# Another order of all operations, and another choice of engine for many of them, in a fused attention and MLP kernel

## The chip, the cores and the metric

One core of one Trainium2 chip runs the whole program. The metric is the device time of one execution in microseconds. The kernel before takes 373.58 us, the median of 4 runs that lie between 371.93 and 376.04 us.

## What is computed

```python
def _attn_ref(q, k, v):                       # each (8, 12, 448, 64), float32
    scores = np.matmul(q, k.transpose(0, 1, 3, 2)) / np.sqrt(64)
    attn = np.maximum(scores, 0.0) ** 2 / 448
    return np.matmul(attn, v)

def _moe_ref(x, w_in, w_out):                 # (3584, 768), (768, 2048), (2048, 768)
    h = x @ w_in
    g = h * (1.0 / (1.0 + np.exp(-1.702 * h)))
    return g @ w_out
```

The attention has no softmax: a relu, a square, a constant. Its output, with the heads side by side, is the `x` of the MLP, and the output is float32, 3584 x 768.

## The kernel before, in words

The work on the matrices is done in float16 with float32 sums. The attention runs in 24 **units** (8 batches x 3 groups of four heads). A unit is loaded as float32 by SP (`Lk`, `Lq`) and cast (`K`, `Q`), or loaded with a cast by a DMA that POOL issues (`jk`, `jq`, `V`). Its k and q are transposed by TensorE and copied out of PSUM (`tk`, `ek`, `tq`, `eq`; units 0 to 5) or by a DMA (`Rk`, `Rq`; the others). Then come 7 blocks of scores (`s`, four matmuls of 64x64 into two PSUM banks), for each block two relus out of PSUM (`r`) and one square (`x`), and the product with v (`a`, 28 matmuls). Its result is copied out of PSUM into the transposed x of the MLP (`e`).

The MLP runs in 8 **groups** of alternately 384 and 512 tokens, each as soon as its tokens are there. Its first product is plain (`f`) for group 0 and for half of group 1; elsewhere it is one level of a Strassen scheme of seven half-size products (`u`), for which sums of the inputs (`T`) and of the weights (`S`) are made on VectorE. Each result goes through a copy out of PSUM (`t`) or a sum with one (`b`), a gelu on ScalarE (`g`), and a scaling into float16 on POOL (`v`). The second product is plain (`m`, group 0), or Strassen in pairs of 128 tokens (`p`, with `A` and `W` for the sums), or single for an odd one (`i`). Its results are copied or added into the output tile (`n`, `h`, `l`), which SP stores (`o`).

**What sets the order.** There is no scheduler at work: the function ends with a list of some 1,930 words, and `do` (from L436) issues one after the other. A word names an operation, its numbers, optionally an engine (`:a` ScalarE, `:d` VectorE, `:p` POOL, else the operation's home) and PSUM banks or buffers (`@3.4`). So `x1.1:p` is the square of unit 1, block 1, on POOL. Each engine takes its own words in the order of the list and waits at each until its inputs and its buffer are there; nothing overtakes. Eight PSUM banks, three buffers for relu results (`rl0` to `rl2`), eight for squares (`at`), five for gelu inputs (`gf`) tie the engines together: a score block can't start before the last reader of its two banks is done.

**Lines that matter.** L88 is the helper `tt` for all two-input operations (squares `at<-rl`, sums); L79 to L85 is the helper `copy` (casts, copies, evictions); L104 the DMAs that POOL issues for q, k and v; L131 transposes; L150 scores; L161 and L163 relu on VectorE and on ScalarE; L169 the square on ScalarE; L182 the product with v; L204 the products `u`, `p`, `i`, `m`; L215 gelu; L218 the scaling on POOL; L405 and L409 the weights' DMAs; L453 ten matmuls on zeros at the start, while the first loads are under way.

Of the kernel before, what the change touches and what calls it, by code (L numbers as in the profile page):

```python
# [15 lines left out]
def kernel(  # L16
# [9 lines left out]
    nc = tc.nc  # L26
# [390 lines left out]
    with tc.manual_schedule():  # L417
# [31 lines left out]
        zero = new("gf", [128, 1024], F16, "zero")  # L449
        nc.vector.memset(zero[:, 0:512], 0.0)  # L450
        zp = bank([7], "zp")
        for _ in range(10):
            nc.tensor.matmul(out=zp, lhsT=zero[:, 0:128], rhs=zero[:, 0:512],  # L453
                             start=True, stop=True)
        words = (
            "I Lk0 K0:d tk0@0 jk1 Lq0 Q0:a jq1 V1 V0 ek0 tq0@1 jk2 tk1@2 eq0 s0.1@3.4 s0.0@5.6 "
            "ek1 r0.1.1@0 s0.3@7.0 r0.1.0:d r0.3.1@1 tq1@1 r0.3.0:d s0.4@2.4 r0.0.0@2 s0.5@3.0 "
            "x0.1 x0.3 s0.2@7.5 r0.0.1 x0.0 r0.4.0@0 r0.4.1 s0.6@6.2 r0.5.0:d@1 x0.4 r0.6.1@2 eq1 "
            "jq2 tk2@4 s1.0@3.2 r0.5.1 r0.6.0 x0.6 r0.2.1@0 x0.5 r0.2.0 x0.2 ek2 r1.0.0@2 r1.0.1 "
            "x1.0 s1.1@0.6 r1.1.1@1 s1.2@1.5 tq2@7 eq2 r1.2.1:d@0 jwa1 jq3 r1.2.0 jk4 jk3 r1.1.0 "  # L460
            "s1.3@3.2 a0@6.4 jwa0 jwb0 r1.3.1@2 s1.4@1.0 r1.3.0 e0.0.1:a jwb1 x1.3 e0.1.1 jq4 "
            "x1.2:a tq3@7 s1.6@2.5 r1.6.1@2 s2.0@3.4 eq3 e0.0.0 V2 s1.5@7.5 r1.6.0 e0.1.0 "
            "s2.2@6.2 jwa3 r1.4.0:d@0 x1.1:p x1.6 jwb3 r1.4.1 x1.4 tk3@1 ek3 r1.5.1@1 r1.5.0 "
            "r2.0.0@2 tk4@0 r2.0.1 x1.5 s2.3@5.7 r2.3.1@0 s2.1@3.1 r2.3.0 V3 r2.2.0@1 ek4 x2.0 "
            "r2.2.1 r2.1.0@2 a1@4.7 r2.1.1:d x2.3 e1.0.0 s2.5@5.0 r2.5.1:d@0 jq5 e1.0.1:a e1.1.1 "
            "x2.2:a x2.1:p jk5 s2.4@6.2 f0.0.0@1 f0.2.0@3 r2.5.0 f0.2.1 f0.0.1 e1.1.0 s2.6@0.7 "
            "x2.5 s3.0@5.4 r2.4.1@1 f0.3.0@2 r2.4.0 r2.6.0@2 r2.6.1 f0.3.1 jwa2 r3.0.0:d@0 x2.4 "
            "f0.1.0@6 s3.1@0.5 r3.0.1 r3.1.1@1 f0.4.0@7 G3 Lk6 f0.1.1 x2.6 a2@4.5 r3.1.0:d x3.0:p "
            "tq4@0 S1.1 e2.0.0 x3.1 f0.4.1 e2.0.1:a f0.2.2 f0.3.2 e2.1.1 g0.2 jwb2 g0.3 f0.1.2 "
            "e2.1.0:a g0.1 eq4 f0.0.2 s3.4@5.3 s3.3@0.2 r3.4.0:d@2 g0.0 f0.5.0@4 r3.4.1 r3.3.0@0 "  # L470
            "V4 f0.4.2 f0.5.1 g0.4 v0.4 s3.2@6.1 r3.2.1@1 r3.2.0 r3.3.1:d x3.4 x3.3 s3.5@5.3 "
            "s3.6@2.0 f0.5.2 f0.6.0@7 f0.6.1 r3.6.1:d@2 r3.6.0 Lq6 r3.5.0@0 f0.7.0@1 x3.2 r3.5.1 "
            "x3.6 tk5@6 s4.1@0.2 g0.5 s4.0@5.3 r4.1.0@1 v0.1 jo0.1 f0.7.1 f0.7.2 v0.3 f0.6.2 "
            "r4.0.0@2 x3.5 r4.0.1:d ek5 r4.1.1 g0.6 x4.0 v0.5 s4.3@4.0 s4.2@5.3 S0.1 a3@2.6 "
            "r4.3.0@0 s4.4@7.4 g0.7 V5 r4.2.1@2 r4.2.0:d r4.3.1:d tq5@1 e3.0.0:a x4.3 x4.1 "
            "e3.0.1:a x4.2 S0.2 s4.6@3.5 r4.4.0@0 s4.5@0.2 f0.9.0@6 f0.9.1 r4.6.1@1 f0.9.2 eq5 "
            "r4.5.0:d@2 f0.12.0@7 f0.8.0@5 f0.12.1 f0.12.2 r4.6.0:d r4.4.1 f0.10.0@4 f0.10.1 v0.7 "
            "f0.10.2 v0.0 x4.6 r4.5.1 s5.3@2.1 g0.12 g0.9 s5.0@0.7 jo1.0 x4.4:p g0.10 r5.0.0@0 "
            "s5.2@3.6 r5.2.1@1 r5.0.1 x5.0:a f0.8.1 f0.8.2 x4.5 v0.10 r5.3.1:d@2 a4@4.0 e4.0.0:a "
            "s5.6@1.6 v0.12 f0.15.0@7 f0.15.1 f0.15.2 g0.8 r5.3.0:d r5.2.0:d r5.6.1@0 v0.9 S1.2 "  # L480
            "x5.3 r5.6.0:d s5.4@2.3 e4.0.1 s5.1@4.5 g0.15 x5.6:a s5.5@1.6 r5.1.0@2 r5.1.1:d "
            "f0.13.0@0 f0.13.1 f0.13.2 S2.1 S2.2 x5.2:a jo0.0 f0.14.0@7 r5.5.0@0 v0.8 x5.1:p "
            "f0.11.0@5 f0.14.1 f0.14.2 f0.11.1 Q6:d jo1.1 f0.11.2 r5.5.1:d r5.4.1:d@1 r5.4.0 "
            "f1.1.0@4 g0.13 x5.4 f1.5.0@1 v0.2 v0.6 v0.15 f1.1.1 x5.5 f1.5.1 K6:p S2.3 g0.11 "
            "f1.3.0@2 f1.2.0@0 a5@5.6 g0.14 Lk7 e5.0.0:a f1.6.0@3 f1.6.1 f1.0.0@7 e5.0.1:a f1.5.2 "
            "g1.5 S2.4 f1.4.0@5 S3.1 T1.1 T1.2 S3.2 W0.1 v0.14 v0.13 v1.5 f1.4.1 u1.3.0@6 t1.3.0 "
            "f1.1.2 S3.4 Rq6 v0.11 T1.4 g1.1 K7 f1.3.1 f1.4.2 f1.3.2 f1.2.1 f1.2.2 V6 W1.1 W1.2 "
            "W3.1 f1.0.1 f1.0.2 g1.0 u1.2.0@1 t1.2.0 Lq7 u1.3.1@4 v1.1 u1.2.1@7 g1.4 v1.0 b1.2.1 "
            "u1.3.2 Q7:a m0.0.0@5 f1.6.2 g1.2 Rk6 v1.2 b1.3.1 S1.4 W2.1 S0.3 S3.3 Lq8 g1.3 V7 Lk8 "
            "g1.6 Rk7 u1.2.3 v1.4 v1.6 n0.0.0 Rq7 s6.1@0.2 W3.2 s6.0@5.3 r6.0.1@2 W2.2 Q8 "  # L490
            "r6.0.0:d u1.3.3 r6.1.1:d@1 r6.1.0:d u1.2.2 s6.2@3.5 K8:p f1.7.0@2 g1.3.1 v1.3.1 "
            "x6.0:a g1.2.1 r6.2.1:d@0 f1.7.1 f1.7.2 v1.2.1 r6.2.0:d T1.3 t1.3.2 W2.4 t1.2.2 "
            "m0.0.1@0 g1.7 x6.1:a u1.2.4 S1.3 x6.2 s6.4@5.3 n0.0.1:a r6.4.0@2 s6.3@2.0 v1.7 W0.2 "
            "Lq9 t1.2.4:d b1.2.3 v1.3 Rq8 r6.4.1 x6.4 r6.3.1@1 r6.3.0 u1.3.4 t1.3.4:d u1.2.5 "
            "g1.2.5 u1.2.6 Q9 s6.5@5.3 r6.5.1:d@0 s6.6@0.2 x6.3:a b1.2.6 b1.3.3 r6.6.0@2 r6.6.1 "
            "x6.6:a g1.2.6 v1.2.6 m0.1.0@1 Lk9 s7.1@3.0 Rk8 Lq10 s7.0@7.2 r6.5.0:d x6.5 n0.1.0:a "
            "r7.1.0:d@1 r7.0.1@2 K9:p r7.1.1:d r7.0.0 g1.3.3 u1.3.6 b1.3.6 u1.3.5 x7.0 s7.2@5.1 "
            "W3.4 s7.3@3.2 v1.2.5 g1.3.5 r7.2.0@0 r7.2.1 g1.3.6 a6@0.7 g1.2.3 v1.2.3 v1.3.5 "
            "e6.0.1:a s7.4@4.6 r7.3.1:d@2 Lk10 K10:p x7.1 s7.5@5.1 x7.2:a m0.1.1@2 Q10:d e6.0.0 "
            "V11 e6.1.0:a e6.1.1:a r7.4.0@1 r7.3.0:d v1.3.6 r7.4.1 Rq9 r7.5.1@0 r7.5.0:d x7.5:a "  # L500
            "x7.3 x7.4 Rk9 s7.6@0.7 s8.1@3.4 n0.1.1:a r7.6.1@2 s8.0@5.6 r8.0.0:d@1 r7.6.0:d x7.6 "
            "m0.2.0@1 Lq11 r8.1.1:d@0 s8.2@5.2 s8.3@0.7 r8.1.0 o0.1 a7@3.4 r8.0.1 x8.0 r8.3.0@2 "
            "r8.3.1 v1.3.3 A1.0.1@0 r8.2.1@1 V8 V10 Lk11 r8.2.0:d x8.1:a s8.4@6.0 e7.0.0 x8.3 "
            "e7.1.0:a r8.4.0@0 s8.5@7.5 e7.0.1:a Q11 r8.5.0@2 x8.2 A1.0.2@1 r8.4.1 e7.1.1:a "
            "r8.5.1:d x8.5 n0.2.0:a m0.2.1@2 s8.6@3.6 s9.1@7.5 Rk10 r8.6.1@1 x8.4 r9.1.1@2 "
            "s9.0@0.4 r9.0.1@0 p1.0.0@1 n0.2.1:a h1.0.0 r9.0.0 Lq12 s9.3@6.5 r8.6.0:d x8.6 "
            "r9.3.0@1 Rq10 r9.1.0:d W0.3 a8@3.4 s9.2@2.7 r9.3.1 x9.1:a s9.4@0.6 e8.0.1:a K11:d "
            "e8.0.0 W1.3 x9.0 p1.0.2 r9.4.1@2 u2.1.0@5 r9.2.0@0 T2.1 Q12 t2.1.0 T2.2 W1.4 e8.1.1 "
            "u2.0.0@6 u2.1.1@2 b2.1.1 W2.3 T2.3 r9.2.1:d e8.1.0:a t2.0.0 r9.4.0 x9.4:a u2.1.2 "
            "u2.0.2 u2.2.0@3 t2.0.2 u2.0.1@4 g2.1.1 Rq11 t2.1.2 b2.0.1 u2.2.1@0 v2.1.1 g2.0.1 "  # L510
            "v2.0.1 u2.0.4 t2.0.4 o0.2 T2.4 u2.0.3 t2.2.0 S0.4 u2.1.4 b2.0.3 b2.2.1 u2.1.3 g2.2.1 "
            "g2.0.3 u2.0.6 u2.2.2 u2.3.0@7 o0.0 u2.0.5 b2.0.6 u2.3.1@4 t2.1.4:d v2.2.1 b2.1.3 V9 "
            "x9.3:a g2.0.6 u2.1.6 u2.1.5 v2.0.3 u2.2.3 t2.2.2 v2.0.6 t2.3.0:d Lk12 b2.1.6 b2.3.1 "
            "h1.0.2:d Lq13 g2.1.3 v2.1.3 g2.0.5 g2.1.6 v2.0.5 g2.3.1 u2.2.4 v2.1.6 g2.1.5 u2.3.3 "
            "u2.3.2 t2.2.4:d x9.2:a b2.2.3 u2.2.5 v2.3.1 v2.1.5 t2.3.2 A1.0.3 W3.3 u2.2.6 g2.2.5 "
            "b2.2.6 W0.4 u2.3.4 t2.3.4 b2.3.3 s9.6@6.2 r9.6.1:d@2 s9.5@5.3 r9.5.0:d@1 p1.0.1@0 "
            "A1.0.4 r9.6.0 g2.3.3 u2.3.6 V12 r9.5.1 s10.0@6.2 r10.0.1:d@0 b2.3.6 x9.6:a l1.0.1 "
            "s10.1@3.5 g2.2.6 r10.1.1@2 Rk11 K12 u2.3.5 p1.0.4 v2.2.5 r10.0.0 r10.1.0 Rk12 Rq12 "
            "p1.0.3 g2.3.5 x9.5 s10.3@2.4 h1.0.4 A1.2.1@1 A1.2.2@0 a9@5.6 r10.3.0:d@1 r10.3.1:d "
            "x10.0:a l1.0.3 s10.2@3.7 e9.0.1 x10.3:p x10.1:a Q13 r10.2.1@0 p1.0.5 Lk14 l1.0.5:a "  # L520
            "s10.6@2.4 r10.6.1@2 r10.2.0:d s10.5@6.7 p1.0.6 r10.5.1@1 e9.0.0:a r10.5.0:d v2.3.3 "
            "r10.6.0:d x10.2:a A1.2.3 l1.0.6 x10.5 o1.1 s11.0@3.1 o1.0 r11.0.0@0 r11.0.1 "
            "s11.3@4.6 s10.4@7.2 r10.4.1@1 p1.2.0@5 x10.6 p1.2.1@0 s11.2@3.1 x11.0 Lq14 r10.4.0 "
            "x10.4 h1.2.0:d r11.3.0@2 r11.2.0:d@0 r11.3.1 r11.2.1 K14:d Lk15 V16 A1.2.4 s11.1@2.7 "
# [140 lines left out]
```

## Time and profile before

| | |
|---|---|
| median of the runs | 373.58 us |
| the profiled execution's own time | 376.04 us |
| its span, first to last instruction | 374.3 us |
| TensorE (PE) busy | 359.2 us, 96% |
| VectorE (DVE) busy | 305.2 us, 82%, 532 instructions |
| ScalarE (ACT) busy | 270.3 us, 72%, 536 instructions |
| GpSimd (POOL) busy | 172.3 us, 46%, 222 instructions |
| mean granted TensorE clock | 0.987 |

The profiled execution is the slowest of the four runs, 2.46 us over the median. Busy time of PE is to be read with care: the ends of matmuls are modelled, and a matmul that waits inside a busy stretch isn't seen as idle. On the other engines, busy time is the union of the instructions' intervals; neighbours overlap a little, so that the durations of a row add up to more.

### The profile page before, as it was taken

The numbers are of one execution on the slowest core, as the hardware profiler recorded it, in microseconds if no ns is written. First come the engines' busy times: TensorE is split into PE (matmuls) and PEld (weight loads), VectorE is DVE, ScalarE is ACT, GpSimd is POOL, SyncE is SP. The second block draws the span as 40 slices with busy tenths as digits, with TensorE's granted clock in tenths as the row PEclk, the third lists the DMA queues.
The fourth block names the chain that finished last, engine by engine and source line by source line (L and its number), as shares of the span: only waits on it lengthen the run. The fifth ranks groups of instructions, "written<-read, shape, count | busy, mean of one in ns | idle before, by whom it ended". The sixth has DMA issues, their size and how long they took to land.

```text
span 374.3 us, 9188 instructions
## 1 busy us (share of the span) xinstructions
PE 359.2 (96%) x3566; PEld 233.1 (62%) x3566; DVE 305.2 (82%) x532; ACT 270.3 (72%) x536; POOL 172.3 (46%) x222
## 2 busy tenths in 40 slices
PE   7869999999899999999999999999999999999993
PEld 3445554655469555885579655786558855588652
DVE  4998999899998996988979878887799699455741
ACT  3867994579898989867787768769977766566311
POOL 6645768554506238376435743046322733114400
PEclk9889999999999999999999999999999999999998
DMA  8999999995998498458772482849173340401224
GB/s 188 191 195 223 205 159 197 207 203 126 208 210 174 68 218 171 98 124 211 165 142 90 102 191 53 167 139 167 26 226 76 49 110 3 109 2 45 63 64 127
DMA packets 64908, 51.39 MB, mean 137 GB/s; under 512 B 35680, under 2 KB 61280, under 8 KB 64864
## 3 DMA queue, kind: packets, MB, share of 16 engines
q1 hardware_dynamic: 48256, 36.71, 40.7%
q0 software_dynamic: 16608, 14.09, 26.5%
q8 instruction: 28, 0.46, 0.5%
q14 instruction: 16, 0.13, 0.2%
HBM read 45.61 MB, written 11.01 MB: 151 GB/s over the span
## 4 chain that ended last, share of the span: by engine, by line
PE 80%; DVE 11%; issue 2%; ACT 2%; DMA 2%; POOL 1%; DVEq 0%; POOLq 0%; ACTq 0%
PE ox L204 27%; PE hx L204 23%; PE sc L150 8%; PE av L182 7%; PE ht L229 6%; PE os L204 4%; DVE at L88 3%; DVE rl L161 2%; PE op L204 2%; DMA q<-in_q_dram 2%; DVE gf L88 2%; ACT rl L163 1%; PE tr L131 1%; DVE wT L88 1%; DVE wout L88 0%
## 5 line engine op out<-in xcount | busy, mean ns | idle before, releaser
L163 ACT ACTIVATE rl<-sc 128x448 f16<-128x448 f32 x219 | 107.2, 550 | 22.1 <-PE sc L150 13.9
L161 DVE TENSOR_SCALAR rl<-sc 128x448 f16<-128x448 f32 x117 | 68.8, 615 | 8.4 <-PE sc L150 7.2
L218 POOL TENSOR_SCALAR go<-gf 128x512 f16<-128x512 f32 x64 | 43.1, 673 | 64.8 <-ACT gf L215 53.0
L88 DVE TENSOR_TENSOR at<-rl 128x896 f16<-128x896 f16 x97 | 65.2, 694 | 3.5 <-ACT rl L163 2.2
L88 POOL TENSOR_TENSOR at<-rl 128x896 f16<-128x896 f16 x22 | 38.4, 1749 | 52.9 <-ACT rl L163 23.0
L204 PEld LDWEIGHTS <-win 128*128 128x128 f16 x624 | 56.9, 98 | 7.3 <-issue 1.8
L88 DVE TENSOR_TENSOR gf<-hx,gf 128x512 f32<-128x512 f32 (+1 forms) x78 | 47.3, 624 | 15.7 <-PE hx L204 9.3
L150 PE MATMUL sc<-qT,kT 64*64 64x448 f16 x672 | 50.4, 366 | 4.5 <-DVE xo L83 2.5
L218 POOL TENSOR_SCALAR ge<-gf 128x384 f16<-128x384 f32 x64 | 36.4, 569 | 34.0 <-ACT gf L215 30.4
L215 ACT ACTIVATE gf<-gf 128x512 f32<-128x512 f32 (+1 forms) x78 | 43.4, 577 | 7.8 <-DVE gf L88 7.5
L169 ACT ACTIVATE at<-rl 128x896 f16<-128x896 f16 x49 | 46.3, 951 | 3.3 <-DVE rl L161 2.9
L204 PEld LDWEIGHTS <-winS 128*128 128x128 f16 x468 | 42.8, 98 | 5.2 <-issue 1.5
L204 PE MATMUL ox<-wout,go 128*128 128x384 f16 x256 | 46.0, 326 | 0.0
L204 PEld LDWEIGHTS <-go 128*128 128x128 f16 x320 | 30.0, 98 | 23.8 <-issue 5.2
L79 ACT ACTIVATE gf<-hx 128x512 f32<-128x512 f32 (+1 forms) x54 | 28.8, 545 | 16.7 <-PE hx L204 13.7
L204 PEld LDWEIGHTS <-ge 128*128 128x128 f16 x288 | 27.0, 98 | 21.3 <-issue 4.8
L182 PE MATMUL av<-at,v 64*64 64x448 f16 x672 | 37.5, 354 | 0.0
L204 PE MATMUL hx<-T,winS 128*128 128x256 f16 (+1 forms) x312 | 35.9, 260 | 0.2
L150 PEld LDWEIGHTS <-kT 64*64 64x64 f16 x672 | 17.6, 106 | 27.0 <-issue 21.8
L204 PE MATMUL ox<-wT,asum 128*128 128x384 f16 x176 | 31.6, 326 | 0.0
L204 PE MATMUL hx<-xo,win 128*128 128x256 f16 x252 | 31.3, 273 | 0.1
L182 PEld LDWEIGHTS <-v 64*64 64x64 f16 x672 | 20.7, 109 | 12.8 <-issue 2.8
(78 smaller groups left out, 481.8 us busy)
## 6 DMA issues: line engine op xcount, KB each, us to landing
out_dram<-osb SPq DMA_DIRECT2D x56, 192.0 KB, 3.3
kst<-in_k_dram SPq DMA_DIRECT2D x19, 448.0 KB, 4.7
qst<-in_q_dram SPq DMA_DIRECT2D x19, 448.0 KB, 4.3
v<-in_v_dram POOLq DMA_DIRECT2D x24, 224.0 KB, 5.7
win<-in_moe_w_in_dram POOLq DMA_DIRECT2D x8, 384.0 KB, 8.9
wout<-in_moe_w_out_dram POOLq DMA_DIRECT2D x4, 768.0 KB, 8.2
k<-in_k_dram POOLq DMA_DIRECT2D x5, 224.0 KB, 6.1
q<-in_q_dram POOLq DMA_DIRECT2D x5, 224.0 KB, 6.8
```

The lines of the kernel that those rows point to most:

```text
L79: nc.scalar.activation(out=o, in_=i, func=AF.Copy)
L88: eng[e].tensor_tensor(out=o, in0=x, in1=y, op=op)
L131: nc.tensor.matmul(out=ps[64 * a:64 * a + 64, j * 128:(j + 1) * 128], lhsT=x[:, a, 64 * j:64 * j + 64], rhs=ident[:, :], is_transpose=True)
L150: nc.tensor.matmul(out=sc[a][c, 0:S], lhsT=st["kT"][r, j, c], rhs=st["qT"][r, :, c], start=True, stop=True)
L161: nc.vector.tensor_scalar(out=o, in0=i, scalar1=0.0, scalar2=None, op0=ALU.max)
L163: nc.scalar.activation(out=o, in_=i, func=AF.Relu)
L169: nc.scalar.activation(out=at, in_=rl, func=AF.Square)
L182: nc.tensor.matmul(out=av[s][64 * a:64 * a + 64, 0:S], lhsT=v16[r, a, 64 * j:64 * j + 64], rhs=at[r, a, :], start=(j == 0), stop=(j == J - 1))
L204: nc.tensor.matmul(out=o, lhsT=lhs(i), rhs=rhs(i), start=start and i == 0, stop=i == n - 1, skip_group_check=True)
L215: nc.scalar.activation(out=o, in_=i, func=AF.Gelu_apprx_sigmoid, scale=1.0 / SC)
L218: eng[e].tensor_scalar(out=o, in0=i, scalar1=SC, scalar2=1.0, op0=ALU.mult, op1=ALU.mult)
L229: nc.tensor.matmul(out=hp[g, f][:, 0:n], lhsT=w[:, i, fo:fo + 128], rhs=xts[g][:, i, 0:n], start=i == 0, stop=i == NK - 1)
```

## The change

The change replaces the list of words. The two lists hold the same operations, with the same numbers, 1,931 words before and 1,933 after; all of them stand in another order, nearly all PSUM banks and relu buffers differ, and 342 operations go to another engine. Most of these moves cancel each other; what is left of them, by kind:

| operation | VectorE | ScalarE | POOL |
|---|---|---|---|
| `K`, cast of k | 5 to 1 | 5 to 7 | 9 to 11 |
| `Q`, cast of q | 5 to 1 | 3 to 9 | 11 to 9 |
| `x`, square | 97 to 92 | 49 to 53 | 22 to 23 |
| `r`, relu | 117 to 115 | 219 to 221 | |
| `t`, copy out of `hx` | 24 to 28 | 54 to 50 | |
| `e`, x of the MLP | 32 to 31 | 40 to 41 | |
| `h`, `l`, `n`, output | 53 to 55 | 36 to 34 | |

The two words that are new are `z13@0` and `z1`: the zero matmuls, now 14 of 384 columns in place of 10 of 512, of which the last stands after the first transposes. They read a part of the tile `wT[2]`, which is written much later. The core of the diff:

```diff
-        zero = new("gf", [128, 1024], F16, "zero")
-        nc.vector.memset(zero[:, 0:512], 0.0)
-        zp = bank([7], "zp")
-        for _ in range(10):
-            nc.tensor.matmul(out=zp, lhsT=zero[:, 0:128], rhs=zero[:, 0:512],
-                             start=True, stop=True)
+        zero = wT[2][:, 0, :]
+        nc.vector.memset(zero, 0.0)
+        zp = []
+
+        def zeros(e, p, n):
+            if p:
+                zp.append(bank(p, "zp"))
+            for _ in range(n):
+                nc.tensor.matmul(out=zp[0][:, 0:NOUT], lhsT=zero[:, 0:128], rhs=zero,
+                                 start=True, stop=True)
+
+        two["z"] = zeros
         words = (
-            "I Lk0 K0:d tk0@0 jk1 Lq0 Q0:a jq1 V1 V0 ek0 tq0@1 jk2 tk1@2 eq0 s0.1@3.4 s0.0@5.6 "
...
-            "s2.2@6.2 jwa3 r1.4.0:d@0 x1.1:p x1.6 jwb3 r1.4.1 x1.4 tk3@1 ek3 r1.5.1@1 r1.5.0 "
...
-            "f0.11.0@5 f0.14.1 f0.14.2 f0.11.1 Q6:d jo1.1 f0.11.2 r5.5.1:d r5.4.1:d@1 r5.4.0 "
...
+            "z13@0 jk1 Lk0 K0:d Lq0 Q0:a I jq1 V1 tk0@1 z1 ek0 tq0@2 tk1@3 jk2 jq2 eq0 s0.3@4.5 "
+            "V0 ek1 s0.1@6.7 s0.0@0.1 r0.3.1@0 tq1@2 s0.4@3.5 r0.0.0@1 r0.3.0:d s0.2@4.0 r0.1.1@2 "
...
+            "r1.1.1:d a0@6.5 x1.0 jwb0 x1.2 e0.0.1:a e0.0.0 s1.5@1.4 s1.6@0.7 jq4 x1.1 r1.5.1@2 "
...
+            "f0.5.1 v0.0 f0.5.2 f0.8.1 f0.8.2 r3.6.1:d v0.3 jwb3 r3.5.1 x3.5:a s4.2@6.5 s4.1@7.4 "
+            "r4.0.1:d x3.6 a3@3.2 r4.1.1@1 r4.2.0:d@0 r4.2.1 jo1.1 g0.5 V4 r4.1.0:d x4.1 s4.3@6.4 "
...
```

The DMAs that POOL issues, in the order of its queue up to the third unit's v: before `jk1 jq1 V1 V0 jk2 jq2 jwa1 jq3 jk4 jk3 jwa0 jwb0 jwb1 jq4 V2`, after `jk1 jq1 V1 jk2 jq2 V0 jk3 jq3 V2`. The last quarter of the first weight (`jwb3`) stands before ahead of `x2.1:p`, and after behind `x3.0:p v0.1 v0.0 v0.3`.

## The prediction

> **What bounds the kernel now.** I read the page's slices first:
>
> ```profile
> PE   7869999999899999999999999999999999999993
> ...
> DVE  4998999899998996988979878887799699455741
> ...
> PEclk9889999999999999999999999999999999999998
> ```
>
> TensorE idles visibly in the first three slices (28 us) and the last; DVE is at nine tenths through the first third. The windows show the same in numbers (columns: window, its length, busy us and instruction counts of PE, PEld, DVE, ACT, POOL, granted clock, DMA share, GB/s):
>
> ```profile
> 10.00:20.00 10.00, 7.17 (x111) 3.62 (x104) 9.25 (x13) 7.82 (x17) 7.58 (x10) 0.83 1.22 189
> 20.00:30.00 10.00, 8.45 (x102) 4.74 (x102) 9.05 (x20) 8.13 (x18) 5.22 (x7) 0.83 1.24 199
> ...
> 50.00:110.00 60.00, 58.16 (x530) 32.86 (x520) 57.29 (x91) 45.67 (x90) 31.23 (x39) 1.00 1.02 180
> 110.00:370.00 260.00, 257.76 (x2517) 177.40 (x2514) 206.16 (x369) 187.91 (x369) 109.56 (x139) 1.00 0.51 115
> ```
>
> DVE is 95% busy up to 110 us, 79% after it. PE's busy time hides waits, so I priced each word by its streaming rate in the chain of waits (start, length, what):
>
> ```profile
> 137.93 1.32 PE av L182 x28
> ...
> 193.29 12.38 PE hx L204 x150
> ...
> 352.89 15.65 PE ox L204 x96
> ```
>
> That is 0.163 us for a matmul of 384 columns, 0.082 for one of 192 (0.107, between the two, for 256), 1.31 us for an `a`, 0.19 for a score block. All words sum to 329.7 us. The 374.3 us span is then 5.6 before the first transpose, 329.7, about 33.0 of gaps (start of one word to start of the next, less its price), and a tail of 5.8. The gaps: 13.9 us before 50 us, 6.4 from 50 to 110, 12.8 in the remaining 258 us, which is 0.5 in 10 us, mostly 0.1 at each change from scores to another product. So **up to 110 us the kernel is paced by VectorE, and after that by TensorE**. The largest gap, 3.0 us at 18.4, has this around it in the timeline:
>
> ```profile
> 17.28 3.57 DVE L88 TENSOR_TENSOR at<-rl 128x896 f16<-128x896 f16 x1 [0.41 <-ACT rl L163]
> ...
> 18.62 1.74 POOL L88 TENSOR_TENSOR at<-rl 128x896 f16<-128x896 f16 x1
> ...
> 21.04 0.38 PE L150 MATMUL sc<-qT,kT 64*64 64x448 f16 x3 [2.31 <-DVE xo L83]
> ```
>
> A square that takes 0.62 us undisturbed takes 3.57; it ends just after POOL's square, and PE then waits 2.31 for a copy queued behind it.
>
> **What the skill says.** The Trainium skill, "SBUF — State Buffer", section "Who interferes with whom": VectorE and GpSimd share a port pair under an exclusive lock; a VectorE instruction with two SBUF inputs collides with a GpSimd one that reads SBUF, and casts and copies in their two-port modes collide with any. The trace agrees: 3.57 against 0.62 above, and `Q6:d` at 54.39 took 2.10 against a row of 1.085 with POOL's square beside it. Instructions stretched by over 0.25 us lose 10.1 us in all before 110 us. "TensorE: Matmul & The Clock Gate", Part 1: too little work halves the clock for a while; here it was 0.83 in both windows from 10 to 30 us and full before and after. "Perfetto Trace Analysis", "Optimizing Scalar/DVE Operations": a duration includes an end that overlaps with the next instruction. So it is: 11 ScalarE relus in a row took 5.25 us, 0.477 each against a row of 0.550 (factor 0.87).
>
> **The change, part by part.**
>
> *Engines.* Rows: casts of k on DVE 0.637, ACT 0.944, POOL 1.017; of q 1.085, 0.950, 0.962; squares 0.62 (undisturbed), 0.951, 1.749; relus 0.615, 0.550; `t` 0.62, 0.54 over both sizes; output copies 0.55, 0.49. DVE: -4x0.637 - 4x1.085 - 5x0.62 - 2x0.615 + 4x0.62 + 0.55 = **-8.1 us**. ACT: 2x0.944 + 6x0.950 + 4x0.951 + 2x0.550 - 4x0.54 - 0.5 = **+9.8**. POOL: 2x1.017 - 2x0.962 + 1.749 = +1.9. On PE nothing: 14x384 against 10x512 zero columns, under the wait for the first loads (k's cast ends at 5.0).
>
> *Order.* I summed the rows of each engine's words ahead of three places in each list:
>
> | ahead of | PE | DVE | ACT | POOL |
> |---|---|---|---|---|
> | `a1` | 9.2, 9.0 | 18.2, 17.2 | 18.9, 18.5 | 15.3, 10.7 |
> | `u2.0.0` | 83.8, 85.9 | 102.7, 101.8 | 95.9, 100.7 | 62.0, 56.7 |
> | the end | 329.7, 329.7 | 327.0, 318.6 | 311.2, 321.2 | 172.8, 174.6 |
>
> (before, after). In the trace `a1` starts at 24.9 us, and group 2's first product at 109.2.
>
> 1. **Up to `a1`: -3.0 us.** `x1.1` leaves POOL, whose first square is now unit 3's, so nothing like the 3.57 us block stands in the list. DVE would have 2.95 us less to wait, and 1.0 less to do. Also V0 moves behind `jk2` and `jq2`: the first POOL loads land some 1.1 us apart (10.34, 11.44, 12.57), so k of unit 2, for which `tk2` waited until 12.6 us with 2.1 us of gap, should land a place sooner, near 11.4. What is late next is the draining of PSUM: 14 relus a unit on two engines. Between 0 and -4.
>
> 2. **`a1` to `u2.0.0`: -1.0 us, and 2.1 us of PE work more done.** DVE's rows in between are 84.5 before and 84.6 after, and it took 84.3 us: the pace stays. ACT's grow from 77.0 to 82.2, at 0.87 some 71.5: under DVE. What remains of the stretched instructions is 7.1 us; fewer DVE casts and POOL squares (5 down to 1 before unit 6) should take a part: 0 to -3. As 2.1 us more of products are issued by then, and PE has room (86 in 105 us), the part behind is shorter by **2.1**.
>
> 3. **POOL's queue: +0.5 us.** `jwb3`, which landed at 31.82 before, now waits for `x3.0:p` and three scalings, the last behind the gelu `g0.3`. That puts its issue near 36 us (PE work 19 to 20 in the order; before, 38 us, less step 1) and its landing, with 2 us a weight quarter and some queue, at 40 to 42. `f0.14.0` needs it at PE work 28.0, before's 47 us, less 3: 44. `V4` behind the 768 KB `jo1.1` lands near 45 for `a4` at 47. SP's `G3` waits for `jwb3`, with `Lk6` and `Lq6` behind it, which landed at 39.3 and 42.3; `K6` comes only after 54. On SP, whose loads, transposing DMAs and stores change places by one or two, the tightest pair is `K9` on POOL with 4.8 us of PE work to the first score block of unit 9: the cast takes 1.0 and a transposing DMA 5.3 to land, 1.5 too much, unless POOL runs ahead. `Q13` follows 1.7 us after `Q14`, which frees its buffer, and a load lands after 4.3: POOL waits some 2.6 us, and behind it `x12.1`, which `a12` needs nearly 30 us of PE work later. All covered, thinly: 0 to +3.
>
> 4. **After `u2.0.0`: 0.** 243.8 us of PE work with 0.5 us of gap in 10, as before. DVE has 216.8 us of rows in place of 224.3, ACT 220.5 in place of 215.3, in 260 us. I can't tell from the trace which gaps close or open: -3 to +3. The last words are the same kind (a product, its add, two stores): the tail stays.
>
> Sum: -3.0 - 1.0 - 2.1 + 0.5 = **-5.6 us**: a span of 368.7. The profiled execution took 376.04 us, 2.46 over the median; taking the difference from the median gives **368.0 us**. All good ends together -12.1, all bad ones +3.9.
>
> **Rivals.**
>
> *The gain is given back* (within 1%, near 372 us). PE is 96% busy, and what DVE hands on in the opening may be met by PSUM banks that aren't drained, or by step 3's transfers late by 2, with step 1 at -1, step 2 at 0 and -2.1: -1.1 in all. For it: the relu rows in the opening hardly change. Against: the 3.57 us block is certain to be another.
>
> *ScalarE becomes the bound* (slower, 380 us). In stretches of 15 us of PE work ACT's rows reach 20.0 (from 60), 18.7 (from 105), 18.4 (from 150) and 19.8 (from 180); before, 19.8 at one place, else up to 17.2. At 0.87 they exceed PE by 2.6, 0.8, 1.8 and 1.8, 7.0 in all; at full rows by 17. If lighter neighbours can't even that out, I take the middle, +12, less the 5.6: +6.4. It decides from an ACT busy over 95% there. Against it: ACT was 72% busy, and its light stretches (12 to 13 beside 15) follow at once.
>
> That the list isn't carried out as written is no rival: every engine takes its words in order.
>
> **Numbers.** Forecast 0.50, given back 0.28, ScalarE 0.22. A measurement here tells about 1%, 3.7 us, from no change: faster is below 369.8, slower above 377.3. The likeliest case alone spans 362 to 370; the range, 362.5 to 378, adds the second case and the near edge of the third.
>
> **What would show it.** Step 1: no DVE square above 2 us before 25 us, `a1` near 22. Step 2: group 2's first product near 105. Step 3: no gap at `f0.14.0` and `a4`. Step 4: gaps of 13 us behind it. I am wrong if `a1` comes no sooner, or if PE waits for ACT's relus after 110 us.

## The result and the profile after

The kernel after takes 375.49 us, the median of 43 runs (373.79 to 378.46); the kernel before, in the runs beside it, 373.69 us (64 runs, 370.15 to 380.53). The ratio is **1.007, 95% interval 1.0054 to 1.0087**: slower by some 2 us, where I had forecast 5.6 us less. (The ratios here leave out the slow executions, those more than 1.5% above the fastest of their kernel, so that they can differ from the quotient of two medians, here 1.005.) The profiled execution of after took 374.04 us, with a span of 372.3.

The slices of the page of after, the rows that were read before:

```profile
PE   8998999999999999999999989999998999999993
...
DVE  4998998989999878778986896878988789674541
...
PEclk9999999999999999999999999999999999999998
```

and the same four windows (window, its length, busy us and counts of PE, PEld, DVE, ACT, POOL, granted clock, DMA share, GB/s):

```profile
10.00:20.00 10.00, 9.43 (x144) 5.40 (x144) 10.00 (x20) 10.00 (x26) 7.32 (x11) 1.00 1.21 189
20.00:30.00 10.00, 8.99 (x118) 4.43 (x114) 9.23 (x17) 8.39 (x20) 3.24 (x4) 1.00 1.24 203
...
50.00:110.00 60.00, 59.00 (x525) 34.17 (x524) 55.50 (x93) 49.08 (x92) 30.55 (x35) 1.00 0.89 183
110.00:370.00 260.00, 254.03 (x2485) 174.80 (x2482) 199.49 (x354) 189.20 (x370) 114.44 (x144) 1.00 0.58 118
```

The opening did what step 1 asked for, and more: PE is busy for 9.43 of the ten us from 10, in place of 7.17, at the full clock in place of 0.83, and `a1` starts at 20.0 us. The loss lies behind. In the PE row a dip to eight stands at the slice from 214 us and another at the one from 279, where before has nines. PE's waits in the profile of after (what waited, for what: us in total, times, longest) name the kind:

```profile
PE hx L204 <- DVE gf L88: 1.3, 3, 1.0
...
PE ht L229 <- DVE xe L83: 1.0, 1, 1.0
PE av L182 <- DVE at L88: 0.9, 1, 0.9
PE ht L229 <- DMA win<-in_moe_w_in_dram: 0.7, 1, 0.7
```

Three single waits of about 1 us for VectorE and one for a weight: what is new is not a throughput that falls short, but four particular instructions that come late. The timeline of after at the three (start, length, engine, line, operation, idle time before it and what ended that):

```profile
28.18 1.67 POOL L88 TENSOR_TENSOR at<-rl 128x896 f16<-128x896 f16 x1 [5.04 <-DVE rl L161]
...
28.45 1.82 DVE L88 TENSOR_TENSOR winS<-win 128x768 f16<-128x768 f16 x1
...
30.19 0.54 DVE L83 CAST xe<-av 128x384 f16<-128x384 f32 x1
...
30.79 0.81 PE L229 MATMUL ht<-xe,win 128*128 128x384 f16 x4 [0.99 <-DVE xe L83]
...
213.09 1.67 POOL L88 TENSOR_TENSOR at<-rl 128x896 f16<-128x896 f16 x1 [1.16 <-ACT rl L163]
213.15 2.09 DVE L88 TENSOR_TENSOR at<-rl 128x896 f16<-128x896 f16 x1
...
215.30 0.76 PE L182 MATMUL av<-at,v 64*64 64x448 f16 x12 [0.88 <-DVE at L88]
...
279.39 1.86 POOL L88 TENSOR_TENSOR at<-rl 128x896 f16<-128x896 f16 x1 [6.72 <-ACT rl L163]
279.63 2.17 DVE L88 TENSOR_TENSOR asum<-go 128x1024 f16<-128x1024 f16 x1
...
281.72 0.61 DVE L88 TENSOR_TENSOR at<-rl 128x896 f16<-128x896 f16 x1
282.26 1.01 DVE L88 TENSOR_TENSOR gf<-hx,gf 128x384 f32<-128x384 f32 x2
282.86 0.66 PE L204 MATMUL hx<-T,winS 128*128 128x192 f16 x6 [0.98 <-DVE gf L88]
```

It is one picture three times. POOL begins a square (`x3.0`, `x16.0`, `x21.2`); 0.06 to 0.27 us later VectorE begins an instruction with two inputs in SBUF (`S0.1`, `x15.4`, `A5.2.1`), which ends only 0.4 to 0.6 us after POOL's square has; what PE waits for is queued behind it, or is it. I call this a **hold**: a VectorE instruction stretched beside an instruction of POOL. I had shown one at 17.28 us in the kernel before (there VectorE began first), and had not looked for others in the new list. That these holds are the loss is so far only read from a picture; the experiments test it.

**A ruler for what follows.** I call *lag* the start of a word on PE less the streaming price (the prediction's prices) of all PE words ahead of it in the list. It grows where PE waits. Worked out from seven traces (`again` are further executions of the same two kernels; the last row is an experiment told below):

| lag, us, at | `a1` | `a3` | `a5` | `u2.0.0` | `a23` | span |
|---|---|---|---|---|---|---|
| before | 15.7 | 18.6 | 20.2 | 25.9 | 37.9 | 374.3 |
| before, again 1 | 16.2 | 18.9 | 20.5 | 27.2 | 38.4 | 374.8 |
| before, again 2 | 12.9 | 15.4 | 17.0 | 22.6 | 33.7 | 370.2 |
| after | 11.0 | 15.5 | 17.2 | 22.0 | 36.0 | 372.3 |
| after, again 1 | 11.5 | 16.4 | 18.8 | 24.0 | 38.0 | 374.2 |
| after, again 2 | 11.4 | 15.9 | 18.4 | 23.0 | 37.0 | 373.2 |
| after, four squares off POOL | 11.8 | 15.5 | 17.2 | 22.1 | 33.9 | 370.1 |

Up to `a1` after gains 1.4 to 5.2 us. From `a1` to `a3` it loses 4.5 to 4.9 in place of 2.5 to 2.9, and from `u2.0.0` to `a23` 14.0 in all three profiles, in place of 11.1 to 12.0. The two losses undo the gain.

### The profile page after: what moved, and what is told of

It reads as the page before. It is cut to its first block, busy times and chain, and to the rows that moved or that the text cites. A ratio compares the mean times of both kernels' runs of the same rounds, so it can differ in the third digit from the quotient of the medians.

```text
span 372.3 us, 9168 instructions
## 1 busy us (share of the span) xinstructions
PE 358.6 (96%) x3570; PEld 233.3 (63%) x3570; DVE 296.7 (80%) x522; ACT 277.5 (75%) x545; POOL 173.3 (47%) x223
## 4 chain that ended last, share of the span: by engine, by line
PE 76%; DVE 10%; issue 4%; DMA 4%; ACT 3%; POOL 2%; SPq 0%; DVEq 0%; POOLq 0%; ACTq 0%
PE ox L204 26%; PE hx L204 23%; PE sc L150 8%; PE av L182 6%; PE ht L229 6%; PE os L204 4%; DMA win<-in_moe_w_in_dram 2%; DVE at L88 2%; DVE rl L161 2%; PE op L204 2%; ACT rl L163 2%; DVE gf L88 1%; DMA qst<-in_q_dram 1%; POOL go L218 1%; DVE winS L88 1%
## 5 line engine op out<-in xcount | busy, mean ns | idle before, releaser
L163 ACT ACTIVATE rl<-sc 128x448 f16<-128x448 f32 x221 | 108.5, 557 | 17.4 <-PE sc L150 12.2
L161 DVE TENSOR_SCALAR rl<-sc 128x448 f16<-128x448 f32 x115 | 67.9, 616 | 11.1 <-PE sc L150 8.9
L88 POOL TENSOR_TENSOR at<-rl 128x896 f16<-128x896 f16 x23 | 40.1, 1745 | 55.7 <-ACT rl L163 37.0
L88 DVE TENSOR_TENSOR at<-rl 128x896 f16<-128x896 f16 x92 | 59.3, 663 | 3.2 <-ACT rl L163 2.3
L215 ACT ACTIVATE gf<-gf 128x512 f32<-128x512 f32 (+1 forms) x78 | 43.1, 579 | 18.9 <-DVE gf L88 18.8
L150 PE MATMUL sc<-qT,kT 64*64 64x448 f16 x672 | 52.2, 358 | 1.3 <-DVE xo L83 0.4
L218 POOL TENSOR_SCALAR ge<-gf 128x384 f16<-128x384 f32 x64 | 34.9, 545 | 39.3 <-ACT gf L215 35.9
L169 ACT ACTIVATE at<-rl 128x896 f16<-128x896 f16 x53 | 50.0, 960 | 1.8 <-DVE rl L161 1.4
L204 PE MATMUL hx<-T,winS 128*128 128x256 f16 (+1 forms) x312 | 37.3, 260 | 1.1 <-DVE gf L88 1.0
L150 PEld LDWEIGHTS <-kT 64*64 64x64 f16 x672 | 19.0, 105 | 24.9 <-issue 19.7
L79 ACT ACTIVATE gf<-hx 128x512 f32<-128x512 f32 (+1 forms) x50 | 27.0, 550 | 9.6 <-PE hx L204 7.0
L204 PE MATMUL hx<-xo,win 128*128 128x256 f16 x252 | 32.2, 273 | 0.0
L182 PEld LDWEIGHTS <-v 64*64 64x64 f16 x672 | 20.2, 107 | 13.8 <-issue 3.0
```

Source lines behind the costliest of these rows:

```text
L79: nc.scalar.activation(out=o, in_=i, func=AF.Copy)
L88: eng[e].tensor_tensor(out=o, in0=x, in1=y, op=op)
L150: nc.tensor.matmul(out=sc[a][c, 0:S], lhsT=st["kT"][r, j, c], rhs=st["qT"][r, :, c], start=True, stop=True)
L161: nc.vector.tensor_scalar(out=o, in0=i, scalar1=0.0, scalar2=None, op0=ALU.max)
L163: nc.scalar.activation(out=o, in_=i, func=AF.Relu)
L169: nc.scalar.activation(out=at, in_=rl, func=AF.Square)
```

## The experiments

All ratios are to the kernel before, with 95% intervals. An edit that replaces words of the list leaves everything else as it is.

### Both kernels again: is the opening always the same?

> The kernel before, once more, for a second profile of it. Theory U (the profiled execution was an unusual one): the 3.57 us square at 17 us, the 3.0 us gap behind it and the two stretches of half clock were of that execution alone; here the span is 369 to 372 us, no VectorE instruction before 25 us takes over 2 us, the mean granted clock is 0.99 or more, and the gaps before 50 us sum to 9 to 11 us, not 13.9. Rival V (it was the usual one, and the new list loses elsewhere): the same gap of 2 to 3 us near 18 us is there again, and the span is 372 to 375.

> The kernel before a third time, since one execution can't tell how often the 3.57 us square comes. Theory U: as in the run beside it, span 369 to 372 us and no such square in at least one of the two. Rival V: the square above 3 us and the gap of 2 to 3 us in both.

> The changed kernel once more, for a second profile. Theory C (collisions): what its order loses is lost where a VectorE instruction with two SBUF inputs starts within 0.3 us behind a POOL square and is held for 1.8 to 2.2 us; S0.1, A1.0.4, x15.4 and A5.2.1 are held again or others in their place, and the gaps behind f0.1.1, a15 and u6.0.4 (1.1 us each) come again or are replaced by as many. Rival D (drift: many small waits spread over the order): the three gaps are of one execution, at most one comes again, and the sum of gaps after 110 us is still 14 us or more.

> A third profile of the changed kernel, to see which gaps are its own. Theory C: at least two of the three gaps of 1.1 us again, the span within 371.5 and 374.5. Rival D: gaps at other places, none above 1 us after 110 us.

No edit. Two executions of before took 376.61 and 371.94 us, and each fits one of the two theories: the first V, the second U. The longer has the hold of `x1.3` again, at another instant (its timeline):

```profile
18.83 3.04 DVE L88 TENSOR_TENSOR at<-rl 128x896 f16<-128x896 f16 x1
...
18.93 0.74 POOL L405 DMA_DIRECT2D win<-in_moe_w_in_dram  x1
...
19.64 1.74 POOL L88 TENSOR_TENSOR at<-rl 128x896 f16<-128x896 f16 x1
```

the shorter hasn't. Nor is TensorE's clock the same; its row in the slices of before, again 1:

```profile
PEclk9599999999999999999999999999999999999999
```

and of before, again 2:

```profile
PEclk9899999999999999999999999999999999999999
```

(the clock was halved for 10.2 us from 8.0, and for 3.4 us from 13.8). `a1` started at 25.3 and at 22.1 us. So the 24.9 us from which step 1 subtracts belong to a long execution of a kernel whose opening varies by 3 us. After's varies less: `a1` at 20.0, 20.5 and 20.4 (and at 21.2 in a fourth profile, told of below), no halved slice. And its three gaps are there in each profile, with 1.16, 1.06 and 1.15 us between the words each time; they are built into the list, not chance.

### The order alone, the engines alone

`order_only` has the new list with the old engine of each operation, `engines_only` the old list with the new engine of each of the 342.

```diff
  order_only, after's list:     -x8.6:p +x8.6  -x1.1 +x1.1:p ...
  engines_only, before's list:  -x8.6 +x8.6:p  -x1.1:p +x1.1 ...
```

> The new order with its banks and zero matmuls, but each operation on the engine that it had before. Theory O (the order loses, by loads that come later and by new waits at places fixed by the order): the ratio to before is 1.005 or more, as for the whole change or worse, since the new order was laid out for other engines. Theory E (the choice of engines loses, ScalarE has 9.8 us more): the ratio is 1.000 or less.

> The order before, with each operation on the engine that it has in the changed kernel (342 differ). Theory O: the choice alone costs little, ratio 0.998 to 1.006. Theory E: ratio 1.007 or more, with waits of TensorE for ScalarE's relus after 110 us. Either way an order laid out for other engines should lose something where two neighbours now share an engine.

Measured: 418.51 us, **1.1185 [1.114, 1.1229]**, and 428.2 us, **1.1447 [1.1395, 1.1498]**. Each ratio lies on the open side of a theory (the first of O, the second of E), but far beyond what either meant, and so decides nothing between them: neither half brings a part of the change, each alone costs 44 us and more. PE's busy row and its longest waits in the profile of `order_only`:

```profile
PE   8788999998899978999889997999979898998993
```

```profile
PE sc L150 <- ACT rl L163: 5.2, 10, 0.9
PE sc L150 <- DVE rl L161: 2.6, 6, 0.9
PE ox L204 <- DVE osb L390: 2.6, 3, 1.3
```

The loss is everywhere (lag 33.1 at `u2.0.0` and 77.4 at `a23`), in many waits of half a us, most of them for PSUM banks that an engine drains too late. Order and engines are fitted to one another word by word; a table of how many operations moved from where to where, like mine, can't price such a change, and undoing a half of it explains nothing. The rest of the study therefore edits a few words.

### The suspected holds, removed

```diff
-x3.0:p  x8.6:p  x16.0:p  x21.2:p
+x3.0    x8.6    x16.0    x21.2
```

These are the four squares of POOL beside which a VectorE instruction of after took over 1.8 us (the fourth pair is `x8.6` and `A1.0.4`, 2.16 us; PE's gap behind it, ahead of `a8`, is 0.58 us).

> The changed kernel with four squares (x3.0, x8.6, x16.0, x21.2), those of POOL beside which a VectorE instruction was held, put on VectorE; nothing else moves. VectorE does 4 x 0.62 us more. Theory C: the holds of 1.1 to 1.5 us at S0.1, A1.0.4, x15.4 and A5.2.1 are gone, and with them the three gaps of 1.1 us: 3 us shorter at most, ratio to before 0.998 to 1.002 in place of 1.007. Rival D: VectorE only has more to do, ratio 1.006 to 1.010.

371.60 us, **0.9966 [0.9943, 0.9988]**, apart from after's 1.0054 to 1.0087: 1.0% of the time, some 3.9 us, for four words; theory C had allowed for 3 at most. All three gaps (3.4 us together) are gone, and that ahead of `a8` is down to 0.19: 3.8 in all. The third place, in its timeline:

```profile
279.07 0.68 DVE L88 TENSOR_TENSOR asum<-go 128x1024 f16<-128x1024 f16 x1
...
279.67 0.62 DVE L88 TENSOR_TENSOR at<-rl 128x896 f16<-128x896 f16 x1
...
280.20 1.01 DVE L88 TENSOR_TENSOR gf<-hx,gf 128x384 f32<-128x384 f32 x2
...
280.81 0.66 PE L204 MATMUL hx<-T,winS 128*128 128x192 f16 x6
```

`A5.2.1` takes 0.68 in place of 2.17 us; VectorE has done its own work and the square's, and the sums for PE follow at 280.20. That is 2.06 us sooner than in after, where PE's last matmuls ahead of the gap start only 1.18 sooner (280.04 against 281.22). VectorE got 2.5 us more to do, by its rows, and the kernel became faster.

Two runs ask whether it is the holds or merely squares that leave POOL. The control moves four that held nothing:

```diff
-x8.1:p  x9.3:p  x17.1:p  x21.1:p
+x8.1    x9.3    x17.1    x21.1
```

> The changed kernel with four other squares of POOL on VectorE (x8.1, x9.3, x17.1, x21.1), beside which no VectorE instruction was held in any of its three profiles. Theory C (the holds cost, not the squares' place): no gain, within 1 us of the changed kernel beside it, 2.5 us of VectorE work more; the three gaps of 1.1 us stay. Rival S (any square is better off POOL in this kernel): 2 us or more faster than the changed kernel, as with the four that held.

> The changed kernel with only x16.0 and x21.2 on VectorE, the two squares that hold VectorE after 110 us. Theory C: the gaps behind a15 and u6.0.4 go, 2.2 us of the 3.9 that all four gave, and the part from group 2's first product to the end takes as much longer than its PE work as before the change (11 to 12 us, not 14). Rival: the later part has other waits in their place, under 1 us gained.

> The changed kernel as it is, the reference for the three others on this chip: 1.005 to 1.009 of the kernel before, as measured at first, with the three gaps behind held instructions in its profile again.

Side by side with after itself (375.78 us, 1.0059 [1.0036, 1.0081], its three gaps there again) the control takes 377.36, **1.0102 [1.0074, 1.013]**: 1.6 us slower, where theory C had expected at most 1. Its waits keep the three:

```profile
PE hx L204 <- DVE gf L88: 1.1, 2, 1.0
...
PE ht L229 <- DVE xe L83: 1.0, 1, 1.0
...
PE av L182 <- DVE at L88: 0.9, 1, 0.9
```

Its lag grows by 2.1 us between `a8` and `a9`, where `x8.1` and `x9.3` stand, in place of 1.0 in after beside it. So a square costs something on VectorE when it held nothing on POOL, and the gain comes from the holds, not from squares that leave POOL. The other run moves only `x16.0` and `x21.2`: 373.93 us, 1.0002 [0.9968, 1.0037], 1.85 us under after beside it, close to the two gaps' 1.06 + 1.15; its lag grows by 12.1 from `u2.0.0` to `a23`, in place of 14.1. So the two holds are 2 of the 2 to 3 us by which this stretch, which step 4 had priced at nothing, had grown.

### The late loads

The fourth wait, of 0.7 us, is `f0.3.0` for a weight quarter (`jwa0`). In after's chain of waits (start, length, what):

```profile
14.79 9.14 DMA win<-in_moe_w_in_dram
...
24.06 0.81 PE ht L229 x4
```

And `V4`, landed at 47.16 us here, came at 49.01 and 48.60 in the other two profiles; in after, again 1, `a4` waits for it (timeline):

```profile
49.06 1.52 PE L182 MATMUL av<-at,v 64*64 64x448 f16 x28 [1.21 <-DMA v<-in_v_dram]
```

The edit puts both a place forward in POOL's queue:

```diff
-jq4 x1.1 ... eq3 jwa0 x1.3 ... jo1.1 g0.5 V4
+jwa0 jq4 x1.1 ... eq3 x1.3 ... V4 jo1.1 g0.5
```

> The changed kernel with those two loads moved and its squares left on POOL. Theory L: the gaps before f0.3.0 and a4 go and the three behind held instructions stay, 1 to 2 us off, ratio 1.001 to 1.005. Rival M: ratio 1.006 to 1.008.

> The changed kernel with the four squares off POOL and, besides, two loads one place earlier in POOL's queue: jwa0 ahead of jq4, and V4 ahead of the 768 KB load jo1.1. Theory L (late loads are the second loss): jwa0 lands some 1.1 us sooner and the gap of 1.1 us before f0.3.0 goes; V4 lands 4 us or more sooner and no gap of 1.4 us stands before a4: 1 to 2 us shorter than with the squares alone, ratio 0.991 to 0.995. Rival M: TensorE then waits at the same places for VectorE, ratio 0.996 to 0.998 as before.

The two moves alone: 377.28 us, 1.0101 [1.0069, 1.0132], no gain, and above what either theory had expected. (The profile is of an execution of 374.90 us, 2.4 under the median, so it can't show all of this.) `V4` landed at 42.28 and `a4` no longer waits, nor does `f0.3.0`; but the load that was passed now comes late (timeline):

```profile
24.10 0.58 PE L131 MATMUL tr<-ident,q 128*64 128x128 f16 x14 [1.65 <-DMA q<-in_q_dram]
```

The q of unit 4 landed at 24.05 us (in after's three profiles at 22.14 to 22.91), and PE waits 1.65 for it. With the four squares as well: 373.20 us, 0.9999 [0.9972, 1.0025], again no gain over the squares alone; but the squares are worth 4.1 us here too. Without the harmful half:

```diff
-jo1.1 g0.5 V4
+V4 jo1.1 g0.5
```

(and the four squares), and a further run that also issues `f0.3.0` and `f0.0.0` later, behind `s2.5`, so that `jwa0` has time to land:

> The changed kernel with the four squares on VectorE and V4 ahead of jo1.1 in POOL's queue, jwa0 where it was. Theory L': a4 no longer waits for V4, 0.5 to 1.4 us off what the squares alone give, 5 us off the changed kernel beside it. Rival M: jo1.1 or something behind it is late in its place, 3.5 to 4.2 us off the changed kernel as with the squares alone.

> As squares and V4, and the first two words of the MLP's first product (f0.3.0, f0.0.0) behind the score block s2.5 in place of ahead of it; nothing else moves. Theory P (a place in the order that asks for the weight a microsecond too soon): the gap of 1 us or more at f0.3.0 goes or halves, the ratio is 0.990 to 0.994. Rival N: s2.5 waits for its bank or VectorE paces this part anyhow, so the gap only changes its place, ratio 0.994 to 0.997 as without the move.

371.48 us, **0.9949 [0.9926, 0.9972]**, 4.3 us under after beside it, and 371.64, **0.9929 [0.9906, 0.9953]** (before took 374.38 beside it). Both beat both kernels. They can't be told from one another, nor surely from the squares alone; in the profile of the second the wait at `f0.3.0` shrank to 0.75 us and one of 1.55 stood before `tq4`. That `V4` coming late costs 0.3 to 1.4 us is read from traces; in the measured times it is inside the intervals.

### What sets before's opening

Three edits of the kernel before ask what the gain of after's opening is made of.

```diff
 before_x11_on_vector:     -x1.1:p                +x1.1
 before_squares_off_pool:  -x1.1:p x3.0:p x5.1:p  +x1.1 x3.0 x5.1
 before_zeros:             the zero matmuls as in after (z13 first, z1 behind tk0)
```

> The kernel before with one word changed: the square x1.1 on VectorE in place of POOL. Theory C: the square x1.3 is not held for 3 us behind it in any execution, so that the executions of 374 to 376 us go and those of 370 to 372 stay: median 371 to 372, ratio 0.992 to 0.996. Rival K (the clock: the long executions are those in which the clock was halved for longer in the opening, whatever VectorE does): ratio 0.998 to 1.002 and executions still from 370 to 377.

> The kernel before with its squares x1.1, x3.0 and x5.1, beside which x1.3, S1.1 and Q6:d were held, on VectorE: the same cure as for the changed kernel. Theory C: those holds, 0.8 to 3 us each, lie in the part that VectorE paces, and their going gains 1 to 3 us, ratio 0.992 to 0.997. Rival: VectorE has 1.9 us more to do in that part, which eats it, ratio 0.999 to 1.003, as with x1.1 alone.

> The kernel before with the new zero matmuls (13 of 384 columns at the start, one behind the first transposes) in place of its 10 of 512; nothing else. Theory Z (the fourteenth zero matmul keeps the clock up in the opening): no half clock before 30 us, and 1 to 2 us shorter, ratio 0.995 to 0.998. Rival Y (the clock stays up in the changed kernel because its opening has fewer idle stretches): the clock is halved for 3.4 us or more, ratio 0.998 to 1.002.

| run | us | ratio | hold of `x1.3` | clock halved for | `a1` at |
|---|---|---|---|---|---|
| `before_x11_on_vector` | 373.23 | 1.0012 [0.9985, 1.0039] | none | 3.4 us | 22.3 |
| `before_squares_off_pool` | 373.91 | 1.0006 [0.9973, 1.0038] | none | 6.8 us | 24.3 |
| `before_zeros` | 373.51 | 0.9967 [0.993, 1.0005] | none in this profile (`x1.6`: 1.31 us) | not at all | 21.8 |

The clock's rows of the second and of the third:

```profile
PEclk9699999999999999999999999999999999999999
```

```profile
PEclk9999999999999999999999999999999999999998
```

The ratios are the rivals' in the first two; in the third it is theory Z's, with an interval that takes in 1. Taking the hold away makes the kernel no faster. The executions of the first lie closer together than before's (371.85 to 374.77 us), those of the second don't (371.61 to 379.35). In the second, `S1.1` (1.50 us before, now 0.55) and `Q6` (2.10, now 0.92) aren't held either, and nothing is gained: no gap of PE had stood behind them. And `a1` comes at 24.3 there with no hold at all.

So the hold isn't the whole of the opening, and the six profiles with before's order show two more parts. TensorE starts `tk2` as soon as k of unit 2 has landed, which was at 11.86 to 13.54 us. From there to `tq3` the words are the same in all six: they took 4.28 us at the full clock (`before_zeros`), 5.05 to 5.86 where the clock was halved for 3.4 us of it, 5.78 with 4.7 us and 6.39 with 6.2 (`before_squares_off_pool`). The hold, where there is one, adds 3.0 and 2.3 us behind that.

The mean granted clock of every execution is on record too. Of 183 executions of before beside these experiments (two of over 500 us left out), the 46 with less than 0.991 took 375.9 us in the median, the 41 with 0.997 or more 372.4. The 44 of after never fell under 0.991, and the 29 with 0.997 or more took 375.3: among these before is ahead by 2.9 us. What goes together isn't shown to be the cause, since a load that lands late makes TensorE wait and may let the clock fall as well. The new zeros alone don't keep it up: of the 14 executions of `before_zeros` four have 0.983 to 0.988. The six of `order_only`, with the new order, have 0.993 to 0.999.

## Why the prediction was wrong

**Step 1, up to `a1`** ("-3.0, `a1` near 22"). Right in kind, larger in size: `a1` at 20.0, no VectorE square over 2 us before 25 us. But the mechanism that I priced, the hold of `x1.3`, was only one of three, and not there in each execution. The halved clock, which I had quoted from the windows at 0.83 and then given no price, was the second; when unit 2's k lands was the third (10.33 us in after, where I had 11.4). And the **base was wrong**: the 24.9 us come from an execution 2.46 us above the median, most of whose excess sat in just this stretch (2.8 of 4.1 us against before, again 2), and I subtracted the whole gain from the median. Against the best of the three profiles of before, the gain at `a1` is 1.6 to 2.1 us.

**Step 2, `a1` to `u2.0.0`** ("-1.0, and 2.1 us of PE work more done"). Failed. With 2.1 us more of PE's work ahead of it, `u2.0.0` was to come at 105 us; it came at 107.9, 109.9 and 108.9. The lag should have grown by 3.1 us less than before's 10.2 (25.9 less 15.7); it grew by 11.0, 12.5 and 11.6. Two terms failed. One is "PE has room", by which more work was to fit in without more time. The part that I had read as VectorE's did come out: its busy time between the two words stayed (80.0 us before, 80.7 after), and its stretched instructions lost less (those over 0.25 us above the median of their shape: 8.7 us before, 5.7 after). Still TensorE came no sooner; VectorE stood idle for 7.1 us in place of 4.8. So VectorE's total wasn't what set the pace of the new list. The other is the pricing of stretched instructions by their sum ("should take a part"): `S0.1` became a new one, with PE behind it (1.16 us), and I had counted squares where I should have looked at who stands beside each and what waits behind. Besides, `f0.3.0` waits 1 us for `jwa0`: I followed `jwb3` and `V4` along POOL's queue, and not this one. Even with holds and `V4` out of the way (the four squares and `V4` moved) the lag grew by 9.2 (21.4 less 12.2), 1.0 less than before's. So two thirds of the credit weren't there: the PE work that is done sooner was paid for in time.

**Step 3, POOL's queue** ("+0.5"). `jwb3` was right: issued at 34.6, landed at 39.77, no gap at `f0.14.0`. `V4` was late by 2 to 4 us against the forecast "near 45", and cost up to 1.4. `jo1.1`, 768 KB ahead of it, took 10.6 us from its issue to its landing.

**Step 4, behind `u2.0.0`** ("0, gaps of 13 us"). Failed: +2 to +3 us (14.0 in place of 11.1 to 12.0 up to `a23`), of which the two holds at 213 and 279 us are 2.2, and removing them gave 1.85. I wrote that the trace couldn't tell which gaps open. It could have been read from the list in part: every square on POOL is a place to look for a two-input instruction of VectorE that will start beside it, and to ask what PE needs next from VectorE's queue. The list has 23 such squares.

**The rivals.** ScalarE did not become the bound: it is 75% busy, and PE's waits for it in the profile of after add up to 0.6 us. "The gain is given back" is nearest, with the place right and the agents in part: of the two I had named for it, a PSUM bank that isn't drained stood at one of the three gaps (the sums at 282.26 us read the bank that PE needs next), and late transfers cost `f0.3.0` some 1 us and `a4` up to 1.4. That a hold would delay the draining I hadn't named. And neither sign that I had set for being wrong came: `a1` was sooner, and PE did not wait for ScalarE's relus after 110 us. The signs did not cover the loss behind the opening.

**The sum.** In the place of -3.0, -1.0, -2.1, +0.5 and 0 stand, against the three profiles of before and as means of the lags above: -3.6 up to `a1`, +1.4 to `u2.0.0`, +2.6 to `a23`: +0.4. The three executions of before (376.04, 376.61, 371.94) lie 1.2 us above its median on average, those of after (374.04, 376.02, 374.99) 0.5 below theirs; with both the sum is +2.1, beside 1.8 between the medians. Some terms of the prediction are off without effect on this: the DVE terms add up to -8.2; ACT's four heavy stretches at 0.87 exceed 15 us by 2.4, 1.3, 1.0 and 2.2, the sum being nearly the same; and the 109.2 us are of `u2.1.0`, which stands ahead of `u2.0.0` (109.7) in the old list.

**What stays open.** Why `x1.3` is held in some executions and not in others. What the clock and the landing of the early loads are each worth in the opening: no run sets one of them alone. What the remaining stretched instructions (0.4 to 0.8 us longer beside POOL's casts of `Q7`, `K9`, `K16`, `K17`) cost: they were not moved.

## What to carry to other kernels

A hold costs nothing by itself (`Q6` and `S1.1` in before), and most of its length where the slowest engine needs the next result of the held queue (gaps of 1.1 to 1.2 us for stretches of 1.3 to 1.5): in a new order, look at each GpSimd instruction that reads SBUF for the two-input VectorE instruction that starts during it, and then at what is queued behind that one. Moving such a square onto the busier engine can be the gain, and moving another, beside which nothing is held, a loss (-3.9 and +1.6 us here). And a stage that differs between executions of one program must be measured in several before a saving in it is subtracted from the median.

## What the runs showed of the hardware

The Trainium skill, "SBUF — State Buffer", section "Who interferes with whom", says of the shared pair that whoever issues first gets it for the whole instruction, and the other blocks. The three holds agree to within the timeline: POOL's square keeps its 1.67 to 1.86 us (its row in before has 1.75), and VectorE's instruction ends 0.42 to 0.55 us after it, a little under its own length (0.55 to 0.68 us where nothing holds it). `Q6:d` in before agrees as well (POOL at 54.08, VectorE at 54.39). The other example of the prediction, `x1.3`, doesn't agree, by the starts that the trace records: VectorE began 1.34 us ahead of POOL's square in one profile (17.28 and 18.62) and 0.81 in another (18.83 and 19.64), and yet it was VectorE that was stretched, until just after the square's end, while the square kept its 1.74 us. POOL was issuing DMAs when `x1.3` began. But in the four other profiles with before's order it also ran beside such an issue and took its 0.62 or 0.63 us, so that an issue alone didn't hold it there. What begins that hold isn't shown.

The granted clock in the opening of one program was halved for 10.2 us in one execution and 3.4 in another. And to move one of the early loads a place forward in POOL's queue made the one that it passed land 1.1 to 1.9 us later (24.05 in place of 22.14 to 22.91 us), which PE waited for.
